# Halved rings for the first layer's weight sums, and a new place and pace for the second layer's

## The chip, the cores and the metric

The kernel runs on one core of one Trainium2 chip. The metric is the device time of one execution in microseconds, as a median over runs. "The trace" is a profile of one execution: each engine's instructions with start and duration, the packets of the DMA engines, and the semaphores by which one engine waits for another.

## The reference, cut to what matters

```python
# batch 8, 8 heads, 576 rows, head size 64, 128 random features, all float32
def phi(x):                                   # x scaled by 64 ** -0.25
    h = einsum('bhsd,md->bhsm', x, omega) - sum(x * x, -1) / 2
    return exp(h - max(h, -1)) / sqrt(128)
kv  = einsum('bhsm,bhsd->bhmd', phi(k), v);  z = sum(phi(k), 2)
x   = einsum('bhsm,bhmd->bhsd', phi(q), kv) / (einsum('bhsm,bhm->bhs', phi(q), z) + 1e-6)
x   = x as (8, 576, 512)                      # 4608 rows of 512
xn  = (x - mean) / sqrt(var + 1e-6) * g_ln
out = x + relu(xn @ w1) @ w2                  # w1 512 x 2048, w2 2048 x 512
```

## The kernel before, in words

The 4608 rows are cut into nine tiles (t = 0 to 8) of 512 rows. For a tile the kernel computes the attention, the layer norm and the two matrix products. A float32 product is done as three float32r products of a rounded part ("high") and what rounding left ("low"): high by high, high by low, low by high.

Tiles 0 and 1 multiply plainly (`mm1`, `mm2`). From tile 2 on (`SEVEN = 2`) the first layer uses a Strassen-like scheme of seven products in place of eight: `seven(t, g, h, between)` computes one step, for group g (0 to 3, one for each 512 columns of w1) and half h (0 or 1, 128 columns of a block of 256). Four of its seven products take sums of weight blocks as their left operand. These sums are made once, while tile 1 runs (`gen_sides`, `halved`, `lesser`), split into high and low, and stored in DRAM (`sides[g, 0]`). From there `gen_ring(i)`, for i = 1 to 4, loads one 512 KB tile for each g: sum i, both halves of columns, high and low. Sum i has one buffer, a tag of w1 that is free by then. `run` in `seven` waits for `("ring", t, g, i)`, multiplies, and frees the buffer after the step with h = 1; the load for the next g can start only then. In a step the products come in the order: a plain one, sum 2, sum 1, sum 3, then what `between` brings (the second layer's products of an earlier step), then a plain one, sum 4, a plain one. A product is six matmuls of 128 x 256.

From tile 7 on (`DEEP = 7`) the second layer uses seven products too. Its weight sums are made by `gen_deep_sides(s)`, s = 0 to 7: four loads of 256 KB from the kept copy of w2 into four `y` buffers (line 505), two additions (line 507), four subtractions (line 514), then two roundings with their stores (`deep_halved`, line 525) and two remainders with their stores (`deep_lesser`, line 534). `gen_rights` loads the seven right operands of each s for tiles 7 and 8 from `kept` or from these stores (line 577), 256 KB each, into some 20 buffers.

There are eight `y` buffers. The tile's activations need them as well: `gen_turned(t, i, ...)` writes a transposed block to DRAM (`way`, line 1202), loads it into a `y` (line 1207), makes differences (line 1226), and `parted` splits these into the operands `ops[t, name]` of the seven products (line 1254). Since there are seven operand places, the operands of tile t + 1 can be written only while the last step of tile t gives them free, and the `y` buffers stay held until then.

The order of the instructions on every engine is settled when the program is built, by `Plan`, a list scheduler. A part of the work is a generator. It yields `wait` (for something done), `get` (a buffer) or `run` (an engine with a cost in us), and then issues its instructions. The part with the lowest rank goes first among those that are ready. For a DMA the planner counts this, and a part that goes on behind a load is taken as ready at `part.end`:

```python
self.free_at[SP] = start + 0.65
part.end = self.dma_at = max(self.dma_at, start + Plan.DMA_LATENCY) + cost   # DMA_LATENCY 2.0
part.end += 1.0                                                              # cost: bytes / 360 GB/s
```

The engines then run their lists in order, and wait on semaphores where the real times differ from the plan. SP issues nearly all the DMAs, in order too.

Of the kernel before, what the change touches and what calls it, by code (L numbers as in the profile page):

```python
# [68 lines left out]
class Plan:  # L69
# [81 lines left out]
    def done(self, key):  # L151
        self.made[key] = self.cur.seen()
        self.wake(lambda w: w == ("wait", key))
# [44 lines left out]
def favor_ffn(ctx, tc, kT, kTr, kD, kDr, vF, vR, qT, qD, omT, gT, w1, w2, out):  # L198
# [21 lines left out]

    def f32(ap):
        return ap.bitcast(F32)

    def act(n, k=1, c=0.09):
        return "run", {ACT: k * (c + 0.00084 * n)}
# [4 lines left out]
    def dve2(n, k=1, c=0.065):  # L230
        return "run", {DVE: k * (c + 0.00105 * n)}, "port"
# [4 lines left out]
    def dma(n):  # L236
        return "run", {SP: n * 4e-6 / 0.36}
# [13 lines left out]
    def wait(*key):  # L251
        return "wait", key
# [187 lines left out]
    def gen_sides(g, k):  # L440


        yield wait("xnT", SEVEN - 1, TC - 1)
        if g + k:
            yield wait("read", *((g, 0) if k else (g - 1, 1)))
        tags, parts = [], []
        for row in (k, k + 2):
            tags.append((yield "get", n_big))
            parts.append(tile_of(tags[-1], [P, 2, HC], F32R))
            yield dve2(DM)  # L450
            w = wparts[1, NK * g + row]
            nc.vector.tensor_tensor(out=f32(parts[-1]), in0=f32(w[:, :, 0]), in1=f32(w[:, :, 1]), op=ALU.add)
        for _ in range(2):
            tags.append((yield "get", n_big))
            parts.append(tile_of(tags[-1], [P, 2, HC], F32R))
        low, high, a, b = parts
        low, high, a, b = f32(low), f32(high), f32(a), f32(b)
        for out, left, right, op in (
            (a[:, 0], low[:, 1], high[:, 1], ALU.add), (a[:, 1], low[:, 0], low[:, 1], ALU.subtract),
            (b[:, 0], a[:, 0], low[:, 0], ALU.subtract), (b[:, 1], high[:, 0], b[:, 0], ALU.subtract),  # L460
        ):
            yield dve2(HC)
            nc.vector.tensor_tensor(out=out, in0=left, in1=right, op=op)
        if (g, 0) not in sides:
            sides[g, 0] = dp.tile([P, 4, 2, 2, HC], F32, tag=f"side{g}", name=f"side{g}", bufs=1)
        done(("read", g, k))
        for n in range(2):
            plan.add(plan.cur.rank, halved(g, k, n, tags[n], tags[2 + n], (a, b)[n]))

    def halved(g, k, n, t_h, t_s, s):  # L470
        hi = tile_of(t_h, [P, 2, HC], F32R)
        eng = yield "run", {ACT: 0.56, DVE: 0.34}
        copy(eng, hi, s)
        plan.add(plan.cur.rank, lesser(g, k, n, t_s, s, hi))
        yield dma(P * DM)
        nc.sync.dma_start(sides[g, 0][:, 2 * n : 2 * n + 2, 0, k], f32(hi))
        yield wait("lo", g, k, n)
        free(t_h)

    def lesser(g, k, n, t_s, s, hi):  # L480
        yield dve2(DM)
        nc.vector.tensor_tensor(out=s.bitcast(F32R), in0=s, in1=f32(hi), op=ALU.subtract)
        done(("lo", g, k, n))
        yield dma(P * DM)
        nc.sync.dma_start(sides[g, 0][:, 2 * n : 2 * n + 2, 1, k], s)
        free(t_s)
        done(("side", g, n, k))

# [2 lines left out]
    def gen_deep_sides(s):  # L491

        f = NK * (s // 2) + s % 2
        yield wait("c22", SEVEN + s // 2, s % 2, 0)
        if s:
            yield wait("deep", s - 1, 1)
        yield wait("kept", f)
        yield wait("kept", f + 2)
        tags, parts = [], []
        for x in (f, f + 2):  # L500
            for i in range(2):
                tags.append((yield "get", n_y))
                parts.append(y_at[tags[-1]].rearrange("p (a c) b -> p a (c b)", a=2))
                yield dma(P * DM)
                nc.sync.dma_start(parts[-1].rearrange("p a b -> p (a b)"), kept[x][:, i])
            yield dve2(DM)
            nc.vector.tensor_tensor(out=parts[-2], in0=parts[-2], in1=parts[-1], op=ALU.add)
        low, a, high, b = parts
        for out, left, right in (
            (a[:, 0], low[:, 1], low[:, 0]), (a[:, 1], high[:, 1], a[:, 0]),  # L510
            (b[:, 0], low[:, 1], high[:, 1]), (b[:, 1], a[:, 1], high[:, 0]),
        ):
            yield dve2(HC)
            nc.vector.tensor_tensor(out=out, in0=left, in1=right, op=ALU.subtract)
        deeps[s] = dp.tile([P, 4, 2, HC], F32, tag=f"deep{s}", name=f"deep{s}", bufs=1)
        for n in range(2):
            plan.add(plan.cur.rank, deep_halved(s, n, tags[2 * n], tags[2 * n + 1], (a, b)[n]))
# [73 lines left out]
        done(("moved", g))  # L591
        free(*n_w[1, NK * g + 1])

    rings = {}

    def gen_ring(i):
        n = (1, 3, 2, 4).index(i)
        (tag,) = n_w[1, NK * (i - 1) + 1]
        for t in range(SEVEN, NT):
            for g in range(NK):  # L600
                yield wait("moved", g)
                for k in range(2):
                    yield wait("side", g, n // 2, k)
                yield "get", (tag,)
                yield dma(2 * P * DM)
                r = tile_of(tag, [P, 2, 2, HC], F32R)
                nc.sync.dma_start(f32(r), sides[g, 0][:, n])
                rings[t, g, i] = tag, r
                done(("ring", t, g, i))

    def column_tiles():
        return slice(0, P // 2), slice(P // 2, P)
# [38 lines left out]
    def gen_k(b, c, kraw, v, early, t_v, n_kp):  # L651
# [103 lines left out]
        def halved_keys(s):  # L755
            t_k = yield "get", n_big
            raw = tile_of(t_k, [P, 4 * P])
            yield dma(4 * P * P)
            nc.sync.dma_start(raw, kD[b - ROUND, c, s] if c < NFULL else kDr[b // 2 - (ROUND + 1) // 2, s])
            t_s = yield "get", n_big  # L760
            ks = tile_of(t_s, [P, 4, P], F32R)
            flat = ks.rearrange("p a b -> p (a b)")
            yield act(4 * P)
            nc.scalar.copy(out=flat, in_=raw)
            yield dve2(4 * P, 1, LOWER)
            nc.vector.tensor_tensor(out=flat[D:P], in0=raw[D:P], in1=f32(flat[D:P]), op=ALU.subtract)
            free(t_k)
            splits[b, c, s] = t_s, ks
            done(("ks", b, c, s))
# [112 lines left out]
    def gen_q2(blk, j, s):  # L882
        rank = plan.cur.rank
        q_turn = yield "get", turn["q"]
        t_q = yield "get", n_big
        qraw = tile_of(t_q, [P, 2 * QB])
        yield dma(P * 2 * QB)
        nc.sync.dma_start(qraw, qD[blk, j, s])
        yield wait("om2")
        t_s = yield "get", n_big  # L890
        qs = tile_of(t_s, [P, 2 * QB], F32R)
        yield act(2 * QB)
        nc.scalar.copy(out=qs, in_=qraw)  # L893
        yield dve2(2 * QB, 1, LOWER)
        nc.vector.tensor_tensor(out=qs[D:P], in0=qraw[D:P], in1=f32(qs[D:P]), op=ALU.subtract)  # L895
        free(t_q, q_turn)
        t_b = yield "get", at_now()

        plan.cur.after = max(plan.cur.after, plan.cur.end + LATE)
        yield us(PE, 0.46)  # L900
        pq = bank(t_b)
        rounded(pq, om_hi, qs, start=True, stop=False)
        rounded(pq, om_lo, qs, start=False, stop=True)
        free(t_s)
        yield from features(blk, j, s, t_b, pq)
# [285 lines left out]
    def gen_turned(t, i, xn, t_n, xn_turn):  # L1191
# [13 lines left out]
        yield dma(P * DM)  # L1205
        xf = y_at[t_f]
        nc.sync.dma_start(xf, way.rearrange("(s f) q x -> (f q) s x", s=4))
        turned[t, i] = t_f, xf
        done(("turned", t, i))

# [154 lines left out]
    def seven(t, g, h, between):  # L1365
# [17 lines left out]

        def ring(i):
            def left(k, l):
                return rings[t, g, i][1][:, l, k, cs]
            return left

        def run(out, i, left, name, start=False):
            if i:  # L1390
                yield wait("ring", t, g, i)
                left = ring(i)
            for j in range(2):
                yield wait("x2", t, name, j)
            yield us(PE, 6 * 0.1134)
            product(out, left, ops[t, name][1], start)
            if i and h == 1:
                free(rings[t, g, i][0])
            if g == NK - 1 and h == 1:
                free(ops[t, name][0])  # L1400

# [399 lines left out]
    for f in SHARED:  # L1801
        plan.add(URGENT, gen_return(f))
    for i in (2, 1, 3, 4):
        plan.add(URGENT, gen_ring(i))
    for part in (gen_ops, gen_parted, gen_staged, gen_xk, gen_p, gen_rights):
        plan.add(URGENT, part())
    for a in range(HOSTS):
        plan.add(URGENT, gen_z(a))
    for s in range(2 * NK):
        plan.add(NS * 3 + 20 * s, gen_deep_sides(s))  # L1810
    plan.add(RK, gen_keys())
    plan.add(RQ, gen_queries())
    plan.add(URGENT, gen_xnT())
# [21 lines left out]
LOWER = 0.19  # L1835
SEVEN, HC = 2, DM // 2
DEEP = 7
SHARED, HOSTS = (4, 5, 6, 7, 2, 3, 0, 1), 8
LENT = (*SHARED, *(f + HOSTS for f in SHARED))
LEAVE, RSIDE = 24, 24  # L1840
# [67 lines left out]
```

## Time and profile before

| what | value |
|---|---|
| median of 3 runs | 936.09 us (935.1 to 940.12) |
| profiled execution, its own time | 938.16 us |
| span in its trace | 936.4 us |
| TensorE busy | 919.0 us, 98% |
| VectorE, ScalarE, GpSimd busy | 84%, 56%, 15% |
| DMA queue, share of 16 engines | 77.0% |

The span runs from the first instruction of the program to the last; the profiled execution took 1.76 us more than its span. Busy time of TensorE (PE) counts a matmul from its start to its modelled end. Matmuls overlap, so the time between two starts is shorter than the duration of one, and an idle time in the views is a little shorter than what was lost.

### The profile page before, as it was taken

Reading aid. Unit: us, or ns where it says so; the run is one execution under the profiler, and the core shown is the slowest. Engines: PE = TensorE matmul, PEld = TensorE weight load, DVE = VectorE, ACT = ScalarE, POOL = GpSimd, SP = SyncE. Lnnn points to the kernel's source line nnn. Section 1 sums busy time; section 2 is a strip of 40 time slices with the busy share of each in tenths; the row PEclk is TensorE's granted clock in tenths of the full one; section 3 lists DMA queues with packets and bytes.
Section 4 is the critical chain, followed back from the end, with each engine's and each line's share of the span. In section 5 each row is a group of like instructions: output and inputs, shape, how many; then the busy total and the mean of one; then the engine's idle time right before and its main releaser. Section 6 shows DMA issues by size and latency. Waiting matters only on the chain.

```text
span 936.4 us, 22910 instructions
## 1 busy us (share of the span) xinstructions
PE 919.0 (98%) x8893; PEld 856.1 (91%) x8893; DVE 789.4 (84%) x1816; ACT 521.2 (56%) x1221; POOL 139.2 (15%) x80
## 2 busy tenths in 40 slices
PE   9999999999999999999999999999999999999998
PEld 7787788888889999999999999999999999999997
DVE  7999998778898888879899779789988787878666
ACT  6677756435665576466655665466735454453342
POOL 3301414100320031001210220022103300000000
PEclk9999999999999999999999999999999999999999
DMA  9179843446787986898989868988689669999992
GB/s 349 67 267 369 278 162 102 151 166 210 242 273 255 337 305 232 304 315 278 314 273 284 307 232 267 345 276 320 239 288 329 233 233 303 325 315 300 319 331 81
DMA packets 125995, 247.60 MB, mean 264 GB/s; under 512 B 11328, under 2 KB 54464, under 8 KB 125888
## 3 DMA queue, kind: packets, MB, share of 16 engines
q1 hardware_dynamic: 125888, 246.15, 77.0%
q8 instruction: 70, 1.15, 0.5%
q14 instruction: 37, 0.30, 0.1%
HBM read 204.16 MB, written 41.94 MB: 263 GB/s over the span
## 4 chain that ended last, share of the span: by engine, by line
PE 79%; DVE 12%; DMA 7%; ACT 1%; issue 1%; DVEq 0%; ACTq 0%
PE b L1360 26%; PE b L1607 22%; PE b L1279 13%; PE b L1639 5%; DMA w<-side 4%; PE b L730 3%; PE b L1085 3%; PE b L779 2%; DVE wide L390 1%; PE b L820 1%; PE b L327 1%; DVE w L376 1%; DVE wide L934 1%; DMA way<-wide 1%; DMA w<-way 1%
## 5 line engine op out<-in xcount | busy, mean ns | idle before, releaser
L1607 PE MATMUL b<-w,hid 128*128 128x256 f32 x1920 | 238.3, 276 | 0.0
L1607 PEld LDWEIGHTS b<-w,hid 128*128 128x128 f32 x1920 | 228.0, 188 | 2.5
L931 POOL PARTITION_ALL_REDUCE wide<-wide x72 | 138.1, 1940 | 601.6 <-ACT wide L241 298.6
L1360 PE MATMUL b<-xnT,w 128*128 128x256 f32 x1344 | 176.1, 277 | 4.2 <-DMA w<-side 2.6
L1360 PEld LDWEIGHTS b<-xnT,w 128*128 128x128 f32 x1344 | 163.3, 188 | 7.0 <-issue 3.3
L1360 PE MATMUL b<-w,w 128*128 128x256 f32 x1008 | 128.4, 276 | 3.6 <-DVE hid L1451 1.5
L1360 PEld LDWEIGHTS b<-w,w 128*128 128x128 f32 x1008 | 121.3, 188 | 6.2 <-DVE hid L1451 1.7
L1423 DVE TENSOR_TENSOR w<-b,w 128x256 f32<-128x256 f32 x224 | 108.6, 485 | 21.5 <-PE b L1360 14.8
L1279 PE MATMUL b<-w,hid 128*128 128x512 f32 x384 | 96.8, 391 | 0.0
L1279 PE MATMUL b<-xnT,w 128*128 128x512 f32 x360 | 89.3, 390 | 0.1
L1279 PEld LDWEIGHTS b<-w,hid 128*128 128x128 f32 x384 | 70.4, 188 | 14.3 <-issue 0.3
L1449 ACT ACTIVATE hid<-w 128x256 fp32r<-128x256 f32 x85 | 43.9, 517 | 67.5 <-DVE w L1423 33.1
L1279 PEld LDWEIGHTS b<-xnT,w 128*128 128x128 f32 x360 | 66.5, 188 | 14.5 <-issue 1.0
L794 ACT ACTIVATE kp<-kp,mb 128x128 f32<-128x128 f32 x176 | 64.0, 396 | 21.6 <-DVE mb L791 21.4
L1451 DVE SCALAR_TENSOR_TENSOR hid<-w,hid 128x256 fp32r<-128x256 f32 x85 | 49.6, 584 | 12.6 <-ACT hid L1449 11.8
L939 ACT ACTIVATE wide<-wide 128x512 f32<-128x512 f32 x72 | 45.1, 632 | 26.4 <-DVE wide L934 25.9
L1639 PE MATMUL b<-w,wide 128*128 128x256 f32 x420 | 54.3, 275 | 0.0
L241 ACT COPY wide<-b 128x512 f32<-128x512 f32 x70 | 40.1, 586 | 23.5 <-PE b L1279 7.9
L934 DVE TENSOR_TENSOR wide<-wide,wide 128x512 f32<-128x512 f32 x64 | 48.7, 768 | 4.3 <-POOL wide L931 4.2
L1639 PEld LDWEIGHTS b<-w,wide 128*128 128x128 f32 x420 | 50.6, 188 | 0.1
L893 ACT CAST wide<-wide 128x512 fp32r<-128x512 f32 x56 | 34.2, 620 | 23.5 <-DMA wide<-qD 19.1
L895 DVE TENSOR_TENSOR wide<-wide,wide 64x512 fp32r<-64x512 f32 x56 | 42.4, 762 | 3.5 <-ACT wide L893 1.9
(162 smaller groups left out, 1408.4 us busy)
## 6 DMA issues: line engine op xcount, KB each, us to landing
w<-side SPq DMA_DIRECT2D x112, 512.0 KB, 6.8
w<-kept SPq DMA_DIRECT2D x80, 512.0 KB, 4.8
w<-kept SPq DMA_DIRECT2D x68, 256.0 KB, 6.4
w<-w SPq DMA_DIRECT2D x32, 512.0 KB, 6.5
wide<-qD SPq DMA_DIRECT2D x56, 256.0 KB, 4.9
w<-deep SPq DMA_DIRECT2D x47, 256.0 KB, 6.4
wide<-kD SPq DMA_DIRECT2D x40, 256.0 KB, 5.6
kept<-w SPq DMA_DIRECT2D x16, 512.0 KB, 2.9
```

The costliest lines, as they stand in the source:

```text
L794: nc.scalar.activation(out=kp[:, j], in_=kp[:, j], func=AF.Exp, scale=1.0, bias=mb[:, j : j + 1])
L895: nc.vector.tensor_tensor(out=qs[D:P], in0=qraw[D:P], in1=f32(qs[D:P]), op=ALU.subtract)
L931: nc.gpsimd.partition_all_reduce(mx, qc, P, bass_isa.ReduceOp.max)
L934: nc.vector.tensor_tensor(out=qc, in0=pq if direct else qc, in1=mx, op=ALU.subtract)
L939: nc.scalar.activation(out=qc, in_=qc, func=AF.Exp)
L1279: nc.tensor.matmul(out.rearrange("p (c a b) -> p c a b", a=AW, b=BW), lhsT, rhs.rearrange("p (a c b) -> p c a b", a=AW, b=BW), start=start ...
L1360: nc.tensor.matmul(passes(out), left(k, l), passes(right[:, r, k]), start=start and k + l + r == 0, stop=k + r == 2, skip_group_check=True,)
L1423: nc.vector.tensor_tensor(out=out, in0=left, in1=right, op=ALU.add)
L1449: nc.scalar.activation(out=hl[:, 0, cols], in_=x, func=AF.Relu)
L1451: nc.vector.scalar_tensor_tensor(out=hl[:, 1, cols], in0=x, scalar=0.0, in1=f32(hl[:, 0, cols]), op0=ALU.max, op1=ALU.subtract)
L1607: nc.tensor.matmul(accs[i].rearrange("p (c a b) -> p c a b", a=AW, b=BW)[:, :, n * 8 : n * 8 + 8], hl[:, l, cs], w[:, r, n * HC : (n + 1) ...
L1639: nc.tensor.matmul(out.rearrange("p (c a b) -> p c a b", a=8, b=8), left[:, l, chunk * P : (chunk + 1) * P], right[:, r].rearrange("p (a c ...
```

## The change

1. The stores of the first layer's sums are laid out by halves: `sides[g, 0]` goes from `[P, 4, 2, 2, HC]` (sum, high or low, row, 256 columns) to `[P, 4, 2, 2, 2, P]` (sum, half h, high or low, row, 128 columns). A store writes pieces of 512 bytes where it wrote 1 KB.
2. Each ring buffer of 512 KB is split into two of 256 KB, `r{i}0` and `r{i}1`, with a load for each half, a wait for each half, and each freed after its own step.
3. `gen_deep_sides(s)` starts at the first step (g = 0, h = 0) of tiles 2, 2, 3, 3, 4, 4, 5, 5 (before: at g = 0 and g = 1 of these tiles, at h = 0). It waits until s - 1 has issued its loads (`begun`), where it waited until the sums of s - 1 were stored. Its rank is 72 + s; before it was 96 + 20 s.
4. `behind_load(t)` makes the planner take a part as ready t us later than the load's planned end: 4 us for the loads of `gen_deep_sides`, 1.5 us for those of kD, qD and `way`. It issues no instruction; it only moves what comes behind these loads to a later place in the engines' lists.

```diff
+    def behind_load(t):
+        plan.cur.after = max(plan.cur.after, plan.cur.end + t)
...
-            sides[g, 0] = dp.tile([P, 4, 2, 2, HC], F32, tag=f"side{g}", name=f"side{g}", bufs=1)
+            sides[g, 0] = dp.tile([P, 4, 2, 2, 2, P], F32, tag=f"side{g}", name=f"side{g}", bufs=1)
...
+    def stored_side(g, k, n, l):
+        return sides[g, 0][:, 2 * n : 2 * n + 2, :, l, k]
...
-        nc.sync.dma_start(sides[g, 0][:, 2 * n : 2 * n + 2, 0, k], f32(hi))
+        nc.sync.dma_start(stored_side(g, k, n, 0), f32(hi).rearrange("p n (h c) -> p n h c", h=2))
...
     def gen_deep_sides(s):
...
-        yield wait("c22", SEVEN + s // 2, s % 2, 0)
+        yield wait("c22", *AFTER[s])
         if s:
-            yield wait("deep", s - 1, 1)
+            yield wait("begun", s - 1)
...
+            if x > f:
+                done(("begun", s))
+            behind_load(4)
             yield dve2(DM)
             nc.vector.tensor_tensor(out=parts[-2], in0=parts[-2], in1=parts[-1], op=ALU.add)
...
+    def gen_split(i):
+        (tag,) = n_w[1, NK * (i - 1) + 1]
+        yield wait("moved", i - 1)
+        yield "get", (tag,)
+        both = tile_of(tag, [P, 2, 2, 2, P], F32R)
+        for h in range(2):
+            r_at[i, h] = both[:, h]
+            free(f"r{i}{h}")
+
+    def gen_ring(i, h):
...
-                yield "get", (tag,)
-                yield dma(2 * P * DM)
-                r = tile_of(tag, [P, 2, 2, HC], F32R)
-                nc.sync.dma_start(f32(r), sides[g, 0][:, n])
-                rings[t, g, i] = tag, r
-                done(("ring", t, g, i))
+                tag = yield "get", (f"r{i}{h}",)
+                yield dma(P * DM)
+                r = r_at[i, h]
+                nc.sync.dma_start(f32(r), sides[g, 0][:, n, h])
+                rings[t, g, i, h] = tag, r
+                done(("ring", t, g, i, h))
...
             nc.sync.dma_start(raw, kD[b - ROUND, c, s] if c < NFULL else kDr[b // 2 - (ROUND + 1) // 2, s])
+            behind_load(1.5)
...
         nc.sync.dma_start(qraw, qD[blk, j, s])
+        behind_load(1.5)
...
         nc.sync.dma_start(xf, way.rearrange("(s f) q x -> (f q) s x", s=4))
+        behind_load(1.5)
...
-                yield wait("ring", t, g, i)
+                yield wait("ring", t, g, i, h)
...
-            if i and h == 1:
-                free(rings[t, g, i][0])
+            if i:
+                free(rings[t, g, i, h][0])
...
-        plan.add(NS * 3 + 20 * s, gen_deep_sides(s))
+        plan.add(NS * 2 + 8 + s, gen_deep_sides(s))
...
+AFTER = [(t, g, 0) for t, g in ((2, 0), (2, 0), (3, 0), (3, 0), (4, 0), (4, 0), (5, 0), (5, 0))]
```

## Rows read from the trace of the kernel before

**Rows 1.** The page: span, busy time of the engines, and their waits' share.
```profile
span 936.4 us, 22910 instructions
PE 919.0 (98%) x8893; PEld 856.1 (91%) x8893; DVE 789.4 (84%) x1816; ACT 521.2 (56%) x1221; POOL 139.2 (15%) x80
PE 79%; DVE 12%; DMA 7%; ACT 1%; issue 1%; DVEq 0%; ACTq 0%
```
**Rows 2.** Waits of TensorE: line, releaser, us in total, times, longest.
```profile
PE b L1360 <- DMA w<-side: 3.4, 7, 0.7
PE b L1360 <- DVE hid L1451: 1.5, 1, 1.5
PE b L1360 <- DVE w L1423: 1.4, 1, 1.4
PE b L1360 <- DVE w L1254: 1.2, 1, 1.2
...
PE b L1360 <- ACT w L241: 0.2, 1, 0.2
```
**Rows 3.** Timeline around the start of tile 7: start, us, instruction, idle before it.
```profile
787.08 1.52 PE L1360 MATMUL b<-w,w 128*128 128x256 f32 x12
789.31 0.92 PE L1360 MATMUL b<-w,w 128*128 128x256 f32 x6 [0.71 <-DMA w<-side]
```
**Rows 4.** The chain that ended last, tiles 7 and 8: start, us, what.
```profile
784.84 9.47 DMA w<-side
796.04 2.04 PE b L1639 x18
798.08 2.72 PE b L1360 x24
800.80 2.04 PE b L1639 x18
802.84 2.04 PE b L1360 x18
804.88 2.04 PE b L1639 x18
806.92 2.72 PE b L1360 x24
```
**Rows 5.** DMA issues of the page: count, KB each, median us to landing.
```profile
w<-side SPq DMA_DIRECT2D x112, 512.0 KB, 6.8
...
wide<-qD SPq DMA_DIRECT2D x56, 256.0 KB, 4.9
w<-deep SPq DMA_DIRECT2D x47, 256.0 KB, 6.4
wide<-kD SPq DMA_DIRECT2D x40, 256.0 KB, 5.6
kept<-w SPq DMA_DIRECT2D x16, 512.0 KB, 2.9
...
side<-wide SPq DMA_DIRECT2D x32, 256.0 KB, 2.5
```
**Rows 6.** Stretches: PE, PEld, DVE, ACT, POOL busy, clock, DMA share, GB/s.
```profile
200.00:262.00 62.00, 62.00 (x387) 51.03 (x386) 54.76 (x131) 32.85 (x68) 9.87 (x5) 1.00 0.68 221
...
781.00:858.00 77.00, 75.46 (x660) 74.76 (x659) 62.63 (x163) 35.28 (x94) 0.00 (x0) 1.00 0.98 328
858.00:936.00 78.00, 71.99 (x623) 70.79 (x621) 51.55 (x125) 27.37 (x71) 0.00 (x0) 1.00 0.72 243
```
**Rows 7.** Timeline of tile 4, 523 to 528 us.
```profile
523.61 0.69 DVE L507 TENSOR_TENSOR w<-w,w 128x512 f32<-128x512 f32 x1 [3.27 <-DMA w<-kept]
...
527.34 1.64 PE L1360 MATMUL b<-xnT,w 128*128 128x256 f32 x12 [1.42 <-DVE w L1423]
```
**Rows 8.** Chain before the wait at the start of tile 3.
```profile
356.54 6.36 DMA wide<-kD
...
364.65 0.34 DVE w L1226
...
366.92 1.19 DVE w L1254
```
**Rows 9.** SP's queue around the end of tile 4 (loads of L505).
```profile
508.64 0.42 SPq L505 DMA_DIRECT2D w<-kept  x1
...
514.40 0.51 SPq L505 DMA_DIRECT2D w<-kept  x1
...
565.68 0.37 SPq L505 DMA_DIRECT2D w<-kept  x1
...
569.07 0.38 SPq L505 DMA_DIRECT2D w<-kept  x1
```
**Rows 10.** The lines of `gen_deep_sides`: loads, additions, stores, with first and last start.
```profile
L505 SPq DMA_DIRECT2D w<-kept x32: 319/423/1651, 263.8 to 770.4; - x32
...
DMA to landing us min/median/max: 3.4/6.1/9.2
L507 DVE TENSOR_TENSOR w<-w,w x12: 670/681/692, 339.5 to 776.3; 128x512 f32<-128x512 f32 x12
L514 DVE TENSOR_TENSOR w<-w,w x24: 384/416/426, 296.8 to 785.4; 128x256 f32<-128x256 f32 x24
L534 SPq DMA_DIRECT2D deep<-w x16: 359/384/604, 303.4 to 793.1; - x16
```

More of the change, by code (lines that the diff above doesn't have):

```diff
@@ L484, in lesser @@
         yield dma(P * DM)
-        nc.sync.dma_start(sides[g, 0][:, 2 * n : 2 * n + 2, 1, k], s)
+        nc.sync.dma_start(stored_side(g, k, n, 1), s.rearrange("p n (h c) -> p n h c", h=2))
         free(t_s)
@@ L592, in gen_move @@
         free(*n_w[1, NK * g + 1])
-    rings = {}
-    def gen_ring(i):
+    rings, r_at = {}, {}
+    def gen_split(i):
[7 more added lines that the diff above has]
+    def gen_ring(i, h):
         n = (1, 3, 2, 4).index(i)
-        (tag,) = n_w[1, NK * (i - 1) + 1]
         for t in range(SEVEN, NT):
@@ L1385, in left @@
             def left(k, l):
-                return rings[t, g, i][1][:, l, k, cs]
+                return rings[t, g, i, h][1][:, l, k]
             return left
@@ L1803, in favor_ffn @@
     for i in (2, 1, 3, 4):
-        plan.add(URGENT, gen_ring(i))
+        plan.add(URGENT, gen_split(i))
+        for h in range(2):
+            plan.add(URGENT, gen_ring(i, h))
     for part in (gen_ops, gen_parted, gen_staged, gen_xk, gen_p, gen_rights):
```

## The prediction, made before the result was known

> **What bounds the kernel now.** I read the page first, then the waits of TensorE, then the chain and the timeline at each wait, and last the DMA rows. TensorE is busy 98% of the span, and the chain of work that ended last lies on it for 79% [rows 1]. The change takes away no matmul, so it can win only the time in which TensorE stands still for want of an operand. The waits of TensorE list nearly all of it behind tile 2: 3.4 us in 7 waits for the rings' loads, one wait each of 1.5, 1.4 and 1.2 us for VectorE, and 0.2 us for ScalarE [rows 2].
>
> Each idle time there is too short. Eighteen matmuls of 128 x 256 take 2.04 us on the chain, 113 ns from start to start [rows 4]. In the timeline twelve of them begin at 787.08 and end by the model 1.52 us later; at 113 ns they were through in 1.36 us, at 788.44, and the next starts at 789.31 [rows 3]. So 0.87 us was lost where 0.71 is shown: 0.16 us is to be added to each wait.
>
> Three places matter. First, the rings: at 784.84 us a load of a sum begins to be issued and takes 9.47 us to land, and the chain runs through it [rows 4]. Second, the waits for VectorE at 366 us (w L1254) and 525 us (w L1423). At 525 us VectorE had stood 3.27 us in front of L507, the addition in `gen_deep_sides`, whose load of `kept` had not landed; TensorE then waited 1.42 us for a sum that VectorE made too late [rows 7]. At 366 us a load of kD took 6.36 us, ScalarE stood in front of it, and the differences L1226 and remainders L1254 of the next tile's operands came last [rows 8]. Third, the `y` buffers: the sums of one s load two pieces at 508.64 and 514.40 and the other two at 565.68 and 569.07 [rows 9]. In between they hold two of the eight `y` over the whole second half of tile 4, when the activations of tile 5 need eight. So part of the activations' differences can only be made at the boundary, where the operands are late already.
>
> **Rings in halves.** What a full buffer allows: it is freed after its product in the step h = 1 and is wanted at the same place of the next step, h = 0. In tiles 7 and 8 a step has 7 x 6 + 6 x 6 = 78 matmuls, 78 x 0.1133 = 8.84 us; the chain shows it, 798.08 to 806.92 [rows 4]. Less the product's own 0.68 us, 8.16 us are left for the planned hand-over, SP's turn and the landing. The median landing is 6.8 us [rows 5], and loads in a crowd take 9.47: too late. A half is wanted two steps after it was freed: 17.68 - 0.68 = 17.0 us. A 256 KB load from `deep`, which has the same 2 KB per partition and goes through the same stretch, lands in 6.4 us in the median [rows 5]; even 9.47 us leaves 7.5 us over. I count all the ring waits as gone: 3.4 + 7 x 0.16 = 4.5 us. Bounds: 0 (DMA so crowded that something else is late) to 4.5.
>
> The price: 112 more issues at SP of 0.37 to 0.51 us each [rows 9]. In a step of 8.84 us of tile 7 SP then issues 6 or 7 right operands and 4 halves, 11 x 0.42 = 4.6 us, which fits. Queued behind a half at SP are `gen_rights` loads, with some 20 buffers ahead of TensorE, or three steps. The waits that TensorE gains are satisfied long before. So nothing on the path.
>
> The stores go to 512-byte pieces. The 32 stores of 256 KB land in 2.5 us [rows 5], and DMA is at 0.68 of its share while the last of them run, with TensorE busy for the whole stretch [rows 6]. Twice the time would be 2.5 us more each; the sums of g = 0 are stored long before tile 2 wants them. Bounds 0 to 2.5 us if the last one were waited for; I take 0.
>
> On the transfers' size the row is set against a rule. Two loads of 256 KB carry what one of 512 KB did, and the row of landings shows 6.4 against 6.8 us [rows 5], so the halves travel in each other's shadow. The Trainium skill, page "DMA: Bandwidth & Descriptors", sections "Anatomy of one DMA" and "Rules for kernel authors", speaks against the change: a transfer costs about 2 us whatever its size, and 1 MiB or more is wanted for most of the rate. By that, were the 2 us not overlapped, tiles 7 and 8 would pay 64 us for 32 more loads; by the row they pay nothing.
>
> **The second layer's sums.** The work itself is unchanged: 4 loads, 4 stores, and on VectorE 2 x 0.68 + 4 x 0.42 + 2 x 0.68 = 4.4 us for each s [rows 10], the remainders counted like the additions, and two roundings. Loads run today from 263.8 to 770.4 us and stores until 793.1 [rows 10], that is, into tile 7, exactly where the ring loads crowd: the share of DMA is 0.98 from 781 to 858 us [rows 6]. After the change the last pair starts with tile 5 (whose start the loads at 565 and 569 us wait for [rows 9]), and 1 MB of stores leaves the start of tile 7. The pair runs at the start of a tile, when all eight `y` are free, and should be through when the activations come for them. The place that becomes late otherwise, the boundary, is relieved.
>
> **Later places behind loads.** The planner counts 2.0 + 0.73 + 1.0 = 3.73 us for a load of 256 KB. The chip shows 4.9 us for qD, 5.6 for kD [rows 5] and 6.1 in the median, 9.2 at most for L505 [rows 10]. With 1.5 us more the plan has 5.23, with 4 us 7.73. So an engine stands less often in front of a load. Of the waits of TensorE that hang on the two edits (366 and 525 us, and the 0.2 us for ScalarE), 1.2 + 1.4 + 0.2 + 3 x 0.16 = 3.3 us can go. Bounds 0 to 3.3; I take 2.7, four fifths, for kD can still land late.
>
> **What can be new.** A new plan moves each of the attention's pieces a little, and a pair of sums puts 4 MB on the DMA queue and 8.8 us on VectorE at the start of four tiles. The nearest rows are single waits of 1.2 to 1.5 us [rows 2]. Bounds: 0 to one at each of four tiles, 4 x 1.6 = 6.4 us; I take 0.6, since VectorE has 7.2 us free in the 62 us before tile 2, and the relu work that TensorE waits for ranks ahead of everything. The wait of 1.5 us for hid L1451 belongs to none of the edits; it may go or stay by chance.
>
> **Sum.** Against the profiled execution: 938.16 - 4.5 - 2.7 + 0.6 = 931.6 us. The median of the runs is 936.09, 2.07 us below the profiled one, so the median to expect is 929.5 us.
>
> **The rivals.**
> - Rings only: their 4.5 us come, but the new plan brings waits like the old ones, so that the 2.7 us are lost and about 1.5 more are paid: 936.09 - 4.5 + 1.5 = 933.1. For it: the waits for VectorE were single events, and each plan has some.
> - No change: DMA itself is the limit of tile 7. For it: the share of 0.98 [rows 6]. Then relief at the rings comes back as a wait for right operands, and the time is about 936. Against it: TensorE is busy 75.46 of these 77 us, and tile 8 with the same bytes has a share of 0.72.
> - Slower by late loads of the sums: VectorE takes its list in order, and the pair's 16 additions (L507) each stand behind a load that lands among the out stores and ring loads of a tile's start, 9.2 us at most against the 7.73 now planned. One such stand cost TensorE 1.42 + 0.16 = 1.6 us [rows 7]. With the rings' gain, six of sixteen decide it: 936.09 - 4.5 + 6 x 1.6 = 941.2. Against it: the margin covers all but the extremes.
> - A cost for each transfer that nothing hides. From the rows: 256 KB stored alone take 2.5 us, 512 KB 2.9 [rows 5], so 2.1 us don't grow with the size. 32 more loads in tiles 7 and 8 would be 67 us of DMA; free are 0.02 x 77 + 0.28 x 78 = 23 us, so 44 us longer, 980. That is the rule of the page named above in this kernel's numbers. Against it: 328 GB/s from 781 to 858 us [rows 6], where lone 256 KB transfers would give 105.
>
> **How the numbers follow.** Half a per cent, 4.7 us, is about what a measurement of this kernel can tell from no change. The forecast has 0.58, rings only 0.24, no change 0.08, late sums 0.08, the cost for each transfer 0.02. Faster by over 0.5% means below 931.4: the forecast's cases and a few of rings only, 0.61. Within 0.5%: the rest of rings only, and no change, 0.30. Slower: 0.09. The likeliest case by itself goes from 926.6 (all of 4.5 + 3.3 won, and 1.6 for L1451) to 931.4. The range also takes in rings only and no change, down to a plain run's scatter: 925.5 to 936.5.
>
> **What would show it.** Right: the waits of TensorE have no row, or under 0.5 us, with w<-side; the last store of the sums lies before 670 us, and the loads of one s lie within some 20 us; L507 no longer stands before a load; DMA's share at the start of tile 7 is lower. Wrong: new waits on TensorE behind 262 us that sum to over 3 us, above all in the first half of tiles 2 to 5; differences L1226 still made at the boundary; waits of L1639 for right operands in tile 7.

## The result, and the profile after

The changed kernel takes 926.43 us in the median of 4 runs (925.38 to 926.62), before 936.49 (935.1 to 940.12): a ratio of 0.9884, 95% interval 0.9855 to 0.9914, or 10.1 us less. The forecast was 929.5, in a range of 925.5 to 936.5. The profiled execution took 925.38 us, with a span of 923.3. One execution each of e1, of e2 and of the kernel before beside them ran in a slow state, at 1139 to 1525 us, and the ratios below leave these three out, the medians don't.

The page after, beside [rows 1], and from its list of groups the two lines of the first layer's products:

```profile
span 923.3 us, 23130 instructions
PE 915.2 (99%) x8893; PEld 855.1 (93%) x8893; DVE 794.7 (86%) x1810; ACT 520.3 (56%) x1227; POOL 139.0 (15%) x80
PE 95%; DVE 3%; DMA 1%; issue 0%; POOL 0%; ACT 0%; DVEq 0%; SPq 0%; ACTq 0%
...
L1380 PE MATMUL b<-xnT,w 128*128 128x256 f32 x1344 | 174.5, 276 | 0.0
...
L1380 PE MATMUL b<-w,w 128*128 128x256 f32 x1008 | 126.7, 276 | 0.2 <-DVE hid L1471 0.2
```

The same two groups in the list of TensorE's groups before (line 1360 there), which names more of the waits than the page does:

```profile
L1360 PE MATMUL b<-xnT,w 128*128 128x256 f32 x1344 | 176.1, 277 | 4.2 <-DMA w<-side 2.6 <-DVE w L1423 1.4
...
L1360 PE MATMUL b<-w,w 128*128 128x256 f32 x1008 | 128.4, 276 | 3.6 <-DVE hid L1451 1.5 <-DVE w L1254 1.2 <-DMA w<-side 0.7
```

Nearly the whole difference between the two traces lies in these two lines. Behind the bars stand busy time, mean, and idle time before. Busy and idle sum to 312.3 us before and to 301.4 after, 10.9 of the 13.1 us by which the span fell. The chain now lies on TensorE for 95%.

The waits of TensorE after, beside [rows 2]. There is none for `w<-side`, none for right operands, and of those for VectorE behind tile 2 only 0.2 us for hid (and 0.6 at the very end) are left:

```profile
PE b L330 <- DVE spin L292: 1.2, 1, 1.2
PE b L1326 <- DVE st L1039: 0.8, 1, 0.8
PE b L1326 <- ACT xnT L1288: 0.7, 1, 0.7
PE b L1659 <- DVE kp L1748: 0.6, 1, 0.6
...
PE b L1380 <- DVE hid L1471: 0.2, 1, 0.2
```

DMA issues after, beside [rows 5]; then, beside [rows 10], the stores and loads of the second layer's sums with their first and last start, and the waits of the addition that stood before a load in [rows 7]:

```profile
w<-side SPq DMA_DIRECT2D x224, 256.0 KB, 4.9
...
side<-wide SPq DMA_DIRECT2D x32, 256.0 KB, 3.3
```
```profile
L543 SPq DMA_DIRECT2D deep<-w x16: 360/471/1758, 306.0 to 627.8; - x16
...
L511 SPq DMA_DIRECT2D w<-kept x32: 319/423/1372, 274.7 to 608.8; - x32
...
DMA to landing us min/median/max: 3.7/5.0/6.9
```

Twice as many ring loads land in 4.9 us where they took 6.8. The stores in pieces of 512 bytes take 3.3 us for 2.5. TensorE waits for none of them; VectorE and ScalarE stand 5.3 us in all behind them, where it was 4.4. The last sums are stored at 628 us, not at 793, and their loads land in 6.9 us at most, under the 7.73 us planned for; the addition (line 516 now) waits for none. ScalarE stands far less in front of the loads of qD and kD, first before, then after:

```profile
ACT wide L893 <- DMA wide<-qD: 19.1, 15, 3.6
ACT wide L764 <- DMA wide<-kD: 15.3, 12, 3.1
```
```profile
ACT wide L912 <- DMA wide<-qD: 3.2, 3, 1.6
ACT wide L782 <- DMA wide<-kD: 2.1, 2, 1.6
```

The differences of the next tile's operands no longer run into the tile's start: for tile 5 the last four (line 1246) begin between 545.15 and 546.28 us, where before they began between 567.36 and 571.34 (line 1226).

Stretches of tiles 7 and 8 after, beside [rows 6]. DMA is as full as before in tile 7, and TensorE is busy all the 75 us:

```profile
771.00:846.00 75.00, 75.00 (x664) 75.00 (x663) 60.08 (x156) 35.34 (x97) 0.00 (x0) 1.00 0.99 336
846.00:923.30 77.30, 72.91 (x640) 72.40 (x638) 53.49 (x130) 27.36 (x71) 0.00 (x0) 0.99 0.70 239
```

### The profile page after: what moved, and what is told of

Read it like the earlier page. It is cut to its first block, busy times and chain, and to the rows that moved or that the text cites. A ratio compares the mean times of both kernels' runs of the same rounds, so it can differ in the third digit from the quotient of the medians.

```text
span 923.3 us, 23130 instructions
## 1 busy us (share of the span) xinstructions
PE 915.2 (99%) x8893; PEld 855.1 (93%) x8893; DVE 794.7 (86%) x1810; ACT 520.3 (56%) x1227; POOL 139.0 (15%) x80
## 4 chain that ended last, share of the span: by engine, by line
PE 95%; DVE 3%; DMA 1%; issue 0%; POOL 0%; ACT 0%; DVEq 0%; SPq 0%; ACTq 0%
PE b L1380 29%; PE b L1627 24%; PE b L1299 20%; PE b L1659 8%; PE b L747 4%; PE b L1104 4%; PE b L797 2%; PE b L838 2%; PE b L330 1%; PE b L885 1%; PE b L1326 1%; DMA wide<-qD 1%; DVE v L1703 0%; PE b L1284 0%; DVE kp L1748 0%; DVE x L1041 0%
## 5 line engine op out<-in xcount | busy, mean ns | idle before, releaser
L1659 PE MATMUL b<-w,wide 128*128 128x256 f32 x348 | 45.3, 275 | 0.0
L1659 PEld LDWEIGHTS b<-w,wide 128*128 128x128 f32 x348 | 42.1, 188 | 0.0
L1469 ACT ACTIVATE hid<-b 128x256 fp32r<-128x256 f32 x40 | 15.3, 382 | 46.6 <-PE b L1380 41.9
```

Source lines behind the costliest of these rows:

```text
L1469: nc.scalar.activation(out=hl[:, 0, cols], in_=x, func=AF.Relu)
L1659: nc.tensor.matmul(out.rearrange("p (c a b) -> p c a b", a=8, b=8), left[:, l, chunk * P : (chunk + 1) * P], right[:, r].rearrange("p (a c ...
```

## The experiments

Each ratio is against the kernel before, run beside it on the same chip, where its median was 936.02 us (e1 to e4), 937.38 (e5 to e8) or 937.87 (e9 to e12). Gains and losses in us against the kernel before are the ratio's, not the difference of two medians.

| run | rings | sums | margins | median us | ratio, 95% interval |
|---|---|---|---|---|---|
| e1_rings_only | halves | old | none | 932.27 | 0.9952 (0.9932 to 0.9972) |
| e3_deep_only | full | pairs | none | 933.21 | 0.9973 (0.9956 to 0.9990) |
| e4_behind_only | full | old | all | 962.44 | 1.0283 (1.0254 to 1.0311) |
| e8_margin4_only | full | old | 4 us only | 962.62 | 1.0261 (1.0237 to 1.0286) |
| e2_no_rings | full | pairs | all | 928.94 | 0.9924 (0.9897 to 0.9951) |
| e5_no_margins | halves | pairs | none | 928.34 | 0.9904 (0.9887 to 0.9921) |
| e9_old_sums | halves | old | all | 958.66 | 1.0217 (1.0187 to 1.0248) |
| e6_late_free | halves, freed together | pairs | all | 936.05 | 0.9989 (0.9978 to 1.0001) |
| e7_quarters | two loads a half | pairs | all | 933.69 | 0.9949 (0.9931 to 0.9968) |
| e10_pair_at_g2 | halves | pairs, later | all | 937.68 | 0.9996 (0.9977 to 1.0015) |
| e11_old_rank | halves | pairs, old rank | all | 932.47 | 0.9940 (0.9921 to 0.9960) |
| e12_changed_again | halves | pairs | all | 926.51 | 0.9874 (0.9841 to 0.9907) |

**One part alone, and all but one.** The runs e1 to e5 and e9 put the three parts (rings, place of the sums, margins) together in every way but the two known ones. Against the changed kernel, the old place of the sums is

```diff
-        yield wait("c22", *AFTER[s])
+        yield wait("c22", SEVEN + s // 2, s % 2, 0)
         if s:
-            yield wait("begun", s - 1)
+            yield wait("deep", s - 1, 1)
...
-        plan.add(NS * 2 + 8 + s, gen_deep_sides(s))
+        plan.add(NS * 3 + 20 * s, gen_deep_sides(s))
```

"no margins" takes out the four `behind_load` lines, and "full rings" takes back `gen_ring`, `run`, and the layout of `sides`.

e1, rings alone: 

> The kernel before with the halved rings and their stores alone; the second layer's sums and the planner's margins as before. Theory (a half has two steps, a full buffer one): the waits of TensorE for w<-side, 3.4 us in 7 waits and about 4.5 us lost, are gone, and the time is 4 to 5 us below before, near 932; the waits for VectorE of 1.2 to 1.5 us stay or are replaced by like ones. Rival (DMA is full in tile 7, so the stall moves to another load): the waits for w<-side go and waits of like size for right operands come, time within 1.5 us of before. Rival (each transfer has a price of its own): slower than before.

Measured: 0.48% or 4.5 us less, and no wait for `w<-side`. Waits for VectorE and ScalarE remain behind tile 2, at other places: 2.2 us in 4 waits, for 4.3 in 4. The theory holds, and both rivals fall.

e2, all but the rings: 

> The changed kernel with the full rings of before: the second layer's sums in pairs, and the margins behind loads. Theory: the waits for VectorE at the starts of tiles 3, 4 and 5 go (about 3.3 us), the ring waits in tiles 7 and 8 stay at 3 to 4.5 us, perhaps a little less at the start of tile 7, from which stores have gone: 932 to 934. Rival (the waits at the rings come from the second layer's stores crowding DMA at the start of tile 7, not from the one step's time): the ring waits go here too, and the time is that of the changed kernel, 926 to 928.

Measured: 7.1 us less, more than expected; the ring waits are, in all and one by one:

```profile
PE b L1369 <- DMA w<-side: 1.9, 2, 1.0
...
787.23 1.60 PE L1369 MATMUL b<-xnT,w 128*128 128x256 f32 x12 [0.99 <-DMA w<-side]
...
882.91 1.61 PE L1369 MATMUL b<-xnT,w 128*128 128x256 f32 x12 [0.90 <-DMA w<-side]
```

They fell from 3.4 us to 1.9, and the waits for VectorE behind tile 2 are gone. With the sums moved and no margins (e3) the ring waits are 1.9 us too. But the fall doesn't lie where the rival has it: at the start of tile 7, from which the stores have gone, a wait of 0.99 us stands where there were three with 1.25 in all, and most of the fall is in tile 8, from 1.81 to 0.90 us. And with the sums in their old places and all margins (e4) the trace has 1.7 us of them as well. So it isn't shown that the sums' own traffic delayed the rings; another plan alone changes these waits by this much.

e3, the sums alone: 

> The kernel before with the second layer's sums alone moved (two a tile, a higher rank, started behind the loads of the one before), no margins behind loads, full rings. Theory: the y buffers are free at the tiles' ends, so the waits at 366 and 569 us go, but VectorE still stands before late loads: 0 to 2 us faster, 934.5 to 936.5. Rival (late loads of the sums, without their margin, stall VectorE in the crowd): several waits of VectorE on w<-kept at L507, slower by 2 us or more.

Measured: 2.5 us less, a little more than expected. The ring waits are 1.9 us here too (3 waits), and waits of TensorE for VectorE of 0.6 to 0.8 us remain. What the rival feared is there: VectorE stands 6.3 us in 5 waits before loads of the sums, for 3.3 in one before. But TensorE doesn't pay for it on balance. With the margins besides (e2) VectorE doesn't stand there at all.

e4, the margins alone: 

> The kernel before with the planner's margins alone (4 us behind the loads of the second layer's sums, 1.5 us behind kD, qD and way). Theory: ScalarE and VectorE stand less before loads (ScalarE before qD and kD 34 us in all, VectorE before w<-kept 3.3 us), TensorE's waits at 366 and 525 us go: 1.5 to 3 us faster, 933.5 to 935. Rival (the waits at the tiles' starts come from the y buffers that the sums hold, not from loads in front of the engines): they stay, time within 1 us of before.

Measured: 26 us slower, against both theories. Two places make it: the start of tile 4, where waits of 11.1 us and a lower clock behind them cost some 13 us, and a wait of 13.4 us, the first line here:

```profile
PE b L1646 <- DMA w<-deep: 13.6, 2, 13.4
PE b L1367 <- ACT w L244: 6.3, 1, 6.3
PE b L784 <- DVE kp L807: 2.9, 1, 2.9
```

The second layer's products of tile 7 wait for the last stored sums. SP's queue shows why: the last load of a transposed block for tile 8 into a `y` (line 1213), loads of the sums (line 508), stores (529, 538), and the first loads of the stored sums as right operands (581):

```profile
782.79 1.59 SPq L1213 DMA_DIRECT2D w<-way  x1
...
850.27 1.74 SPq L508 DMA_DIRECT2D w<-kept  x4
858.80 0.89 SPq L529 DMA_DIRECT2D deep<-w  x2
859.79 1.00 SPq L538 DMA_DIRECT2D deep<-w  x2
862.53 0.33 SPq L581 DMA_DIRECT2D w<-deep  x1
```

All four loads of the last sums are issued at 850 us, at the end of tile 7, when the activations of tile 8 give the `y` buffers back. In the old places the sums of s = 7 may start from the second group (g = 1) of tile 5 on, if those of s = 6 are stored, with the rank 236; in this plan the activations of tiles 7 and 8 had the buffers first. What makes the loss at the start of tile 4 isn't shown.

e8, the 4 us margin alone: 

> The kernel before with the 4 us margin behind the loads of the second layer's sums alone (old places, full rings, no 1.5 us margins). The run with all margins and the old places lost 26 us, in one wait of 13.4 us for the last stored sums at the end of tile 7, whose loads came only when the y buffers were freed there, and about 13 us at the start of tile 4. Theory (old places let the sums and the activations compete for y, and any shift of the plan can let the last sums lose): if the 4 us decide who gets the buffers, the last sums come late again, 10 to 26 us slower; if the 1.5 us do, they are in time and the time is within 3 us of before. Rival (the loss comes from the margins by themselves): slower by a few us in many small waits.

Measured: 24 us slower, with the same wait of 13.4 us for `w<-deep` in its trace, which is of an execution 5 us below the median. The four last loads are issued together at 846.69 us. So the margin behind the sums' own loads is enough to let them lose.

e9, halves and margins with the old places: 

> The changed kernel with the second layer's sums in their old places, rank and order (one after the other), halved rings and all margins kept. Theory (with margins and old places the last sums lose the y buffers to the activations of tile 8, as in the two runs with full rings): a wait of 10 us or more for w<-deep at the end of tile 7, 945 to 960. Rival (that loss needs full rings, whose loads crowd DMA): no such wait, 927 to 931.

Measured: 20 us slower, with a wait of 12.4 us for `w<-deep`. So the loss doesn't need full rings.

e5, no margins: 

> The changed kernel without the margins behind loads: halved rings and paired sums. Theory (the parts add up: rings 4.5 us, paired sums 2.5 us of which half is ring waits, margins the rest): no ring waits, some waits of TensorE for VectorE and ScalarE come back, as in the run with the paired sums alone; 929 to 931. Rival (margins help only where rings are full): the time of the changed kernel, 926 to 927.

Measured: 928.34 us, between the two expectations' ranges. In its trace TensorE has no wait of over 0.3 us behind tile 1 until the last 0.6 us; that trace is of an execution of 926.75 us, one of the two fastest, so it doesn't show what the slower ones wait for. ScalarE stands 34.9 us before qD and kD here, as much as before (34.4), and the time is hardly longer. The margins' worth beside halved rings is 1.9 us by the medians, with overlapping intervals; beside full rings (e2 against e3) it is 0.49%, 4.6 us, with intervals that don't meet.

**What in the halves helps.** e6 gives both halves back only after the step h = 1:

```diff
-            if i:
-                free(rings[t, g, i, h][0])
+            if i and h == 1:
+                free(rings[t, g, i, 0][0], rings[t, g, i, 1][0])
```

> The changed kernel with both halves of a ring given back only after the step h = 1, as the full buffer was; the transfers stay halves of 256 KB. Theory (what counts is the second step's time before a half is wanted again): a half for h = 0 is again wanted 8.16 us after it was freed, so waits for w<-side return in tiles 7 and 8, up to the 1.9 us of the run with paired sums and full rings; 927 to 929. Rival (the smaller transfer, landing sooner, is what helps): no waits for w<-side, the time of the changed kernel, 926.4.

Measured: no wait for `w<-side`, as the rival had it, but 936.05 us, as neither had it. The loads of these halves (line 624) take this to land (least, median, most), beside 10.1 us at most for the full rings of before and 9.6 in e2:

```profile
DMA to landing us min/median/max: 2.9/5.7/8.0
```

That is within the 8.16 us that one step leaves. So with the sums moved a transfer of half the size is enough, and the second step is a reserve. The time was lost elsewhere. The plan came out another way, with the next tile's query features ahead of the first products of tile 4, and TensorE waited for VectorE:

```profile
PE b L1299 <- DVE wide L914: 5.1, 1, 5.1
```

Why the plan put these features there isn't settled; the run answers the question on the rings by its waits and not by its time.

**More transfers.** e7 loads each half in two:

```diff
-                nc.sync.dma_start(f32(r), sides[g, 0][:, n, h])
+                for l in range(2):
+                    nc.sync.dma_start(f32(r[:, l]), sides[g, 0][:, n, h, l])
```

> The changed kernel with each half ring loaded by two transfers of 128 KB, 448 loads where it has 224, the same bytes and buffers. Theory (transfers travel in each other's shadow and SP has room): the same time, within 1 us of 926.4, no waits for w<-side. Rival (each transfer has a price of 2 us that nothing hides): DMA in tiles 7 and 8 pays 32 x 2 x 2 us more, waits for w<-side or right operands, 20 us slower and more. Rival (SP's issues are the bound in tile 7, 11 of 0.42 us in a step of 8.84 before): 15 issues take 6.3 us of 8.84, a few us slower.

Measured: 933.69 us, 7 us slower than the changed kernel, so my theory fails at this number of transfers; the rival with 20 us and more fails too. Two waits for `w<-side` are back, in tile 8, of 0.43 and 3.09 us. SP's queue before the longer one:

```profile
897.26 0.85 SPq L625 DMA_DIRECT2D w<-side  x2
...
900.13 4.77 SPq L625 DMA_DIRECT2D w<-side  x4
```

The load that TensorE waited for was issued at 897.26 and landed 7.1 us later, the longest of all loads of the sums in this trace. In the 12.9 us before it SP had been issuing for 11.7. The next four took SP until 904.9. In the waits of SP from 860 to 910 us, line 625 stands 4.5 us before landings of `w<-kept` and 2.5 us before landings of `w<-deep`; in the changed kernel it stands there mostly before TensorE, which has yet to free a half. The DMA engines had room, with 291 GB/s at a share of 0.91 in the ten us before the wait (last section), for 336 at 0.99 in tile 7 of the changed kernel. So the bytes by themselves were not the limit: SP's list came late. How much of the wait is late issue and how much the long landing, the run doesn't separate. The trace is of the slowest execution (935.83 us; the fastest took 928.36). What else it lost lies in waits of 0.7 and 0.4 us at the end of tile 2 and in the lower clock behind the long wait (last section).

**What in the place of the sums helps.** e10 starts the pairs in the second half of the same tiles:

```diff
-AFTER = [(t, g, 0) for t, g in ((2, 0), (2, 0), (3, 0), (3, 0), (4, 0), (4, 0), (5, 0), (5, 0))]
+AFTER = [(t, g, 0) for t, g in ((2, 2), (2, 2), (3, 2), (3, 2), (4, 2), (4, 2), (5, 2), (5, 2))]
```

> The changed kernel with the pairs started in the third group of the same tiles (g = 2 for g = 0), all else as it is. Theory (the y buffers: a pair must be through before the next tile's activations want them): the pair and the activations now want the same buffers in the second half of a tile, differences are made at the boundary, waits of TensorE at the starts of tiles 3 to 6 of 1 to 10 us each, 930 to 950. Rival (only DMA's crowding at the start of tile 7 mattered, and these stores too are gone by 670 us): the time of the changed kernel within 1.5 us.

Measured: 937.68 us, 11 us slower than the changed kernel beside it; the whole gain is gone. TensorE's waits are for the operands of the next tile:

```profile
PE b L1380 <- ACT w L244: 4.7, 2, 3.3
...
PE b L1380 <- DVE w L1274: 1.2, 3, 0.5
```

The chain at the start of tile 4 shows differences (line 1246), remainders (1274) and an addition of the sums (516) on VectorE, one after another, with TensorE behind them:

```profile
463.59 0.33 DVE w L1246
463.92 0.60 DVE w L516
...
466.47 0.33 DVE w L1246
...
467.34 0.41 DVE w L1246
467.75 0.35 DVE w L1274
468.10 0.04 issue
468.14 1.92 PE b L1380 x10
```

That the `y` buffers made them late, and not only VectorE's additional work there, is seen in SP's queue. The last load of a transposed block for tile 4 (line 1226) is issued here in the changed kernel:

```profile
446.42 0.37 SPq L1226 DMA_DIRECT2D w<-way  x1
```

and here in e10, where the blocks were in DRAM as early (the last store to `way` is issued at 436 us), and SP's list stands before this load until a store of the sums has landed, the last of which is issued at 453.42 (line 543):

```profile
453.42 0.38 SPq L543 DMA_DIRECT2D deep<-w  x1
...
458.69 0.38 SPq L1226 DMA_DIRECT2D w<-way  x1
...
SPq L1226 <- DMA deep<-w: 1.3, 1, 1.3
```

e11 keeps the pairs' starts and gives back the old rank:

```diff
-        plan.add(NS * 2 + 8 + s, gen_deep_sides(s))
+        plan.add(NS * 3 + 20 * s, gen_deep_sides(s))
```

> The changed kernel with the old rank of the sums, 96 + 20 s for 72 + s; the pairs' starts and their linking stay. Theory (what counts is that the pair has its y buffers at the start of a tile, which the start condition gives by itself): within 2 us of the changed kernel. Rival (without the rank the activations take the buffers first): the second of a pair is caught at the tile's end, waits at the boundaries or for w<-deep, 5 us or more slower.

Measured: 932.47 us, 6 us slower than the changed kernel beside it, as the rival had it: waits of TensorE of up to 1.6 us at the starts of tiles 3 to 5. The second of the pair of tile 3 loads its last piece at 421.19 us, where the changed kernel does at 406.77, and the last transposed block for tile 4 comes at 454.32, where it was 446.42. The start alone does not give the pair its buffers in time; the rank does its part.

e12, the changed kernel again: 

> The changed kernel itself, on the chip of the three runs beside it, so that they are compared with it directly: 925 to 928, no waits of TensorE for w<-side.

Measured: 926.51 us, no waits for `w<-side`.

## Why the prediction was right, and what was mis-sized

**Rings.** The term was 4.5 us, and the halves alone bring 4.5 us (e1). Of the reason given, the second step that a half has, e6 shows that with the sums moved it wasn't needed: the waits stay away without it, because a half lands in 8.0 us at most. And the 3.4 us were not the full rings' alone: with full rings another plan has 1.7 to 1.9 us of them (e2, e3, e4). In the times no overlap of the parts shows: e1 and e3 bring 4.5 and 2.5 us, and both together 9.0 (e5).

**The price of the transfers.** Nothing on the path, as said, for 224 loads. It held for a reason with an edge: SP had room for 11 issues in a step, and with 15 it was late in tile 8 (e7). The fixed cost of about 2 us for each transfer that the Trainium skill gives, page "DMA: Bandwidth & Descriptors", section "Anatomy of one DMA", shows in no wait at 256 KB; what 128 KB cost, 7 us, is far below 2 us for each. That section is headed as one on transfers that GpSimd issues, which the prediction doesn't say; here SP issues them, so the runs don't test it where it stands.

**The sums.** I gave their move no term of its own; it had its share in the 2.7 us. Alone it brings 2.5 us (e3). The reason, the `y` buffers at a tile's end, is shown by e10, which puts only the start of the pairs half a tile later and loses all: there the next tile's blocks wait for the buffers that the sums hold.

**The margins.** Here the working missed something. I took them as a gain by themselves, and as a rival I had late loads before the addition L507. That engines stand less in front of loads is so: ScalarE 5.3 us for 34.4 before qD and kD, VectorE none for 3.3 before the sums' loads. But with the old places the margins cost 24 to 26 us (e4 and e8 against the kernel before, e9 against e1), and not by late loads: the last sums lose the `y` buffers and are stored a tile too late (e4, e8, e9). With the new place they bring 4.6 us beside full rings and perhaps 1.9 beside halves. That the change sets both at once was luck for this term: the danger of the margins alone stands nowhere in the prediction.

**The sum.** The forecast gain was 6.6 us on the median; 10.1 were measured. The time, 926.43 us, is the lower end of what the prediction calls its likeliest case, 926.6 with everything won. The step that was mis-sized is the one on what is new and what goes by chance. I charged 0.6 us for new waits, and none came; I kept a fifth of the 3.3 us of waits on VectorE and ScalarE, and all went; and I left the wait of 1.5 us for hid to chance, and it fell to 0.2. That is 0.6 + 0.6 + 1.3 = 2.5 of the 3.5 us. Another 0.4 us is the median of before, 936.09 at the forecast and 936.49 with a fourth run. The rest is near what the runs scatter, and its cause isn't shown; the busy time of the two groups of line 1380 fell by 3.3 us, more than the 11 waits' 0.16 us each. The two profiled executions lie 12.8 us apart, 2.7 more than the medians, so this much is the executions' own. A part of it lies in the opening, where both kernels issue the same instructions up to 145 us: before, TensorE waited 1.1 us for kv there, and in the second trace of the changed kernel (e12) another opening wait of 0.9 us is there.

**The signs.** Of the signs of being right that the prediction names, three came: no wait for `w<-side`, the last store of the sums at 628 us and the loads of one s within 16 to 23 us, and no stand before the addition's loads. One didn't: DMA's share at the start of tile 7 isn't lower, 1.04 in its first 39 us for 0.98. So the gain doesn't come from a relieved DMA queue there. The signs of being wrong stayed away: no new waits, no late right operands, and the differences are made before the tile's end.

**The rivals.** "Rings only" is what e1 shows, with the old sums. "No change", since DMA is full in tile 7, is refuted: its share is 0.99 after and TensorE never waits there. The two slower ones didn't come; a danger was there but lay elsewhere, in the order in which buffers are given out.

## What to carry to other kernels

Where two kinds of work share a pool of buffers, first see who holds them at the moment when the bounding engine needs the next set: a background job belongs where the pool is free anyway, and should be given all of it at once and not in two halves across a boundary. An improvement of the planner's estimates is no free edit; by itself, as here, it may turn the order in a shared pool and cost more than all waits that it removes. Splitting a buffer's load in two pays as long as the issuing queue has room, and the next split may not.

## What the runs showed of the hardware

A long wait costs TensorE more than itself. In the run e6, stretches around the wait of 5.1 us (columns as in [rows 6]):

```profile
458.00:464.00 6.00, 1.26 (x12) 1.07 (x10) 4.57 (x10) 4.77 (x13) 2.46 (x2) 1.00 1.06 385
464.00:470.00 6.00, 5.55 (x40) 4.12 (x42) 5.87 (x15) 4.54 (x12) 1.85 (x1) 0.52 0.79 253
470.00:480.00 10.00, 9.66 (x104) 9.27 (x101) 9.44 (x23) 5.89 (x13) 2.28 (x2) 0.95 0.41 136
```

The granted clock is 0.52 of full speed in the six microseconds behind it, near the lower of its two levels, 1.2 for 2.4 GHz, and 0.95 in the ten after. In e4, behind the wait of 13.4 us:

```profile
852.00:866.00 14.00, 0.59 (x6) 0.40 (x5) 7.09 (x17) 1.64 (x4) 0.00 (x0) 0.59 0.55 174
866.00:870.00 4.00, 4.00 (x19) 4.00 (x20) 0.00 (x0) 0.59 (x1) 0.00 (x0) 0.50 0.89 288
870.00:880.00 10.00, 10.00 (x83) 10.00 (x83) 7.45 (x17) 2.74 (x7) 0.00 (x0) 0.92 0.99 333
```

Nineteen matmuls take 4 us in the second stretch, 211 ns each where it was 113. In e7, the ten microseconds before the wait of 3.09 us and the ten around it:

```profile
890.00:900.00 10.00, 10.00 (x85) 9.71 (x84) 6.22 (x16) 4.26 (x11) 0.00 (x0) 1.00 0.91 291
900.00:910.00 10.00, 6.91 (x45) 6.63 (x44) 4.08 (x11) 2.97 (x9) 0.00 (x0) 0.83 0.81 263
```

The kernel before, whose longest wait is 1.5 us, shows 1.00 in every stretch of [rows 6]. I had priced waits at their length alone. What the clock adds, as an estimate from these stretches (the length of those behind the wait, in e7 of the one around it, times what is missing from 1.00), is some 3 us in e6 and e4 and 1.7 in e7.
